# Blockwise-causal attention and routed experts on one core: q and k cast by their loads into a two-head layout, v loaded per head, first expert computed block by block

## The chip, the cores and the metric

The kernel runs on 1 core of one Trainium2 chip. The metric is device time in microseconds (us), as the median of several runs: 352.87 us over 3 runs (350.46 to 354.48) before the change. A core has these engines: TensorE (PE; its weight loads are listed as PEld), VectorE (DVE), ScalarE (ACT), GpSimd (POOL) and SyncE (SP). Transfers between memory (DRAM) and the on-chip SBUF are issued by SP, ACT or POOL and run on 16 DMA engines. A load that also changes the data type is issued by POOL here. TensorE writes to PSUM, from where DVE or ACT take results.

## The reference, cut to what matters

```python
# q, k, v: (8, 8, 576, 64) float32;  batch, heads, positions, head size
scores = matmul(q, k.transpose(0, 1, 3, 2)) / sqrt(64)
mask = (pos[:, None] // 64) >= (pos[None, :] // 64)        # causal by blocks of 64
attn = softmax(where(mask, scores, -1e9))
x = matmul(attn, v)                                        # rows: (batch, position); 8 heads x 64 = 512 columns
# 4608 rows x, domain_id: one of 8 experts per row
for e in range(8):
    rows = domain_id == e
    out[rows] = relu(x[rows] @ w1[e]) @ w2[e]              # w1: 512 x 1024, w2: 1024 x 512, float32
```

All inputs are float32; the kernel computes in float16 with float32 accumulation.

## The kernel before, in words

The program has two stages, each written out in the order in which its instructions are issued (manual schedule; every engine runs its own instructions in that order and waits only for the data and buffers that an instruction needs).

**Attention** (L457 to L546) walks over 32 head pairs, `p` = 0 to 31, four pairs to a batch. `emit_T(p)` (L323) transposes q and k of a pair: 16 PE transposes into one PSUM tile PT, then two DVE copies into the SBUF tile QK (L334 for q, L337 for k). It is called two pairs ahead. `emit_G` (L368) computes transposed scores in three groups, each followed by exponentials on ACT (L366): group 0 is `mm_qk` for the first 128 keys, group 1 the second and fourth, group 2 the third plus twelve small 64x64 matmuls (L388) for the diagonal blocks. `emit_P` and `emit_Q` (L424, L429) multiply with v for the pair before, at L414 and L419; DVE divides by the row sums (L435, L436) and writes the rows x. The sums come from columns of ones in the v tiles `vS` and `VE` (`emit_VE`, L442). After the fourth pair of a batch `store_x` (L449) writes 576 rows to the DRAM tensor `x_rows` over SP.

A partition holds four consecutive positions of a head (1 KB of float32), 128 partitions hold 512 positions. The other 64 positions of q (the first) and of k (the last) are "tails", loaded separately into `ts` and transposed once per batch (`emit_tail`, L343). With four positions per partition, the order of positions inside QK is permuted, and `inverse` (L189) computes permuted row numbers for the gather (the tile `rw`).

Loads arrive as float32 in `qs`, `ks`, `ts` and `vst`, and are then cast to float16 tiles `qh`, `kh`, `th`, `vS`. For batch 0 DVE and ACT cast q, k and tails, and DVE casts v. For all others POOL does (`cast_qk` L111, `cast_t` L118, `cast_v` L132; the casts have the lines L116, L120 and L134). `loads(p)` (L470) places these casts and the next loads on POOL, for two batches at a time, after pair p; the staging tiles have room for two batches, so a load of two batches waits until those before are cast. POOL also issues weights: expert 0 (w1 and w2) after pair 3, w1 of expert 1 after pair 19. A generator `routing()` (L273) interleaves, in chunks after the pairs, the DVE and PE work that finds the rows of each expert (L212 and L220 among it).

**Experts** (L549 to L645): for each of 8 experts, 5 blocks of 128 rows are gathered from `x_rows` by POOL (L556), transposed by PE (L568), multiplied with w1 (`mm1`, L582: 64 matmuls of 320 columns; ReLU on ACT, L588), then with w2 (`mm2`, L597), copied by DVE (L601) and scattered to the output by POOL (L602). Gathers run two experts ahead. Weights are cast by their loads (L139, L142). The gather of the first block waits for the last `x_rows` store. A loop for overflowing experts follows; it isn't entered with these inputs.

## Time and profile before

| what | value |
|---|---|
| median of 3 runs | 352.87 us (350.46 to 354.48) |
| the profiled execution | 349.14 us |
| its span (first to last instruction of the trace) | 347.1 us, 2.04 us less |
| mean granted TensorE clock | 0.888 |
| busy: PE, PEld | 277.5 us (80%), 177.8 us (51%) |
| busy: POOL | 213.5 us (62%) |
| busy: DVE, ACT | 165.8 us (48%), 141.4 us (41%) |
| moved by DMA | 65.03 MB, 187 GB/s over the span |
| read from memory | 67.15 MB |

The profile shows one execution. Busy time is a share of the whole span, over two stages with different limits, so a stage is read by itself: the page cuts the span into 40 slices of 8.7 us with one digit each (tenths of busy time; the clock in tenths; the DMA engines' mean share), and the trace can be asked for any stretch. Bytes moved are counted as written, so a load that casts float32 to float16 counts half of what it reads. A group row gives line, engine, operation, output and input tiles, shapes and count, then busy us and mean ns, then the idle time of the engine just before it. A row in order of time begins with the start and the duration in us; durations of matmuls overlap, and the distance from start to start is what one costs. In a row of waits stand the total, the number of times and the longest.

### The profile page before, as it was taken

How to read it: one execution, taken by the hardware profiler on the slowest of the kernel's cores; microseconds unless marked ns; L12 is line 12 of the kernel's file. 1: busy time of each engine (PE TensorE's matmuls, PEld its weight loads, DVE VectorE, ACT ScalarE, POOL GpSimd, SP SyncE). 2: the span in 40 equal slices, each digit the busy share in tenths (PEclk: the TensorE clock that was granted, in tenths of full speed). 3: DMA queues.
4: the chain of work that ended last, by engine and by line, in shares of the span. 5: the costliest groups of instructions: out<-in, count | busy, mean ns of one | idle time of the engine just before them, and what ended most of it. 6: DMA issues, size and time to landing. Idle time of an engine off the chain costs nothing. (4 is left out here: it accounts for less than half of the span.)

```text
span 347.1 us, 7286 instructions
## 1 busy us (share of the span) xinstructions
PE 277.5 (80%) x3014; PEld 177.8 (51%) x3014; DVE 165.8 (48%) x315; ACT 141.4 (41%) x196; POOL 213.5 (62%) x252
## 2 busy tenths in 40 slices
PE   1567661797977986998329999999999999999990
PEld 1345441565655654765215556474656556564740
DVE  6874991759777783876210332404041322313030
ACT  2544551347474983999203314060513224050500
POOL 9858992975668575100068578887878687703141
PEclk9996885559788996999857999999999999999996
DMA  7999999999938999122225999899998989601121
GB/s 217 250 283 266 313 188 247 190 328 272 266 93 284 274 263 235 27 73 70 68 75 113 195 246 212 241 191 240 180 259 181 255 168 226 213 14 69 66 92 50
DMA packets 29539, 65.03 MB, mean 187 GB/s; under 512 B 4734, under 2 KB 11390, under 8 KB 29504
## 3 DMA queue, kind: packets, MB, share of 16 engines
q0 software_dynamic: 21328, 57.42, 67.7%
q1 hardware_dynamic: 7376, 6.72, 7.0%
q8 instruction: 25, 0.41, 0.5%
q10 hardware_dynamic: 800, 0.39, 0.4%
q14 instruction: 10, 0.08, 0.1%
HBM read 67.15 MB, written 15.20 MB: 237 GB/s over the span
## 5 line engine op out<-in xcount | busy, mean ns | idle before, releaser
L366 ACT ACTIVATE A<-ps 128x1024 f16<-128x1024 f32 (+1 forms) x96 | 82.6, 885 | 67.4 <-PE ps L361 40.8
L588 ACT ACTIVATE hT<-ph 128x640 f16<-128x640 f32 x64 | 45.1, 704 | 118.2 <-PE ph L582 118.2
L582 PE MATMUL ph<-xT,w1h 128*128 128x320 f16 x512 | 72.7, 303 | 0.2 <-DVE xT L571 0.2
L597 PE MATMUL po<-w2h,hT 128*128 128x512 f16 x320 | 70.4, 379 | 0.0
L556 POOL DMA_INDIRECT xg<-x_rows,tok x40 | 40.5, 1012 | 47.4 <-DMA x_rows<-x 34.5
L602 POOL DMA_INDIRECT out_dram<-osb,tok x40 | 40.8, 1020 | 39.7 <-DVE osb L601 26.1
L582 PEld LDWEIGHTS <-w1h 128*128 128x128 f16 x512 | 50.7, 99 | 22.0 <-issue 0.6
L601 DVE COPY osb<-po 128x512 f32<-128x512 f32 x40 | 27.7, 691 | 50.4 <-PE po L597 49.3
L571 DVE COPY xT<-pt 128x512 f16<-128x512 f16 x40 | 15.7, 421 | 73.6 <-PE pt L568 71.4
L597 PEld LDWEIGHTS <-hT 128*128 128x128 f16 x320 | 30.9, 98 | 36.0
L414 PE MATMUL po<-VE,ATE 128*128 128x130 f16 x160 | 34.6, 241 | 18.0 <-DVE x L436 15.2
L419 PEld LDWEIGHTS <-A 128*128 128x128 f16 x640 | 34.3, 107 | 16.9 <-issue 15.9
L361 PE MATMUL ps<-QK 64*128 64x512 f16 (+3 forms) x256 | 39.3, 346 | 1.2 <-ACT ATE L366 0.7
L419 PE MATMUL po<-vS,A 128*128 128x65 f16 x640 | 39.2, 208 | 0.0
L436 DVE TENSOR_TENSOR x<-po,rc 128x768 f16<-128x768 f32 x32 | 30.6, 957 | 3.3 <-DMA x_rows<-x 2.2
L126 POOL DMA_DIRECT2D vst<-in_v_dram x25 | 25.1, 1014 | 10.5 <-DMA qs<-in_q_dram 9.1
L568 PE MATMUL pt<-identh,xg 128*128 128x128 f16 x160 | 15.0, 229 | 14.9 <-issue 9.3
L330 PE MATMUL PT<-identh,qh 128*64 128x128 f16 x256 | 16.1, 261 | 10.7 <-DVE qh L116 8.6
L134 POOL CAST vS<-vst 128x1024 f16<-128x1024 f32 (+1 forms) x21 | 18.2, 897 | 10.0 <-DMA vst<-in_v_dram 7.0
L142 POOL DMA_DIRECT2D w2h<-in_moe_w_dram x32 | 17.4, 562 | 9.2 <-DMA vst<-in_v_dram 6.2
L337 DVE COPY QK<-PT 128x512 f16<-128x512 f16 x32 | 21.8, 680 | 0.0
L414 PEld LDWEIGHTS <-ATE 128*128 128x128 f16 x160 | 16.5, 103 | 10.1 <-issue 7.8
(103 smaller groups left out, 288.7 us busy)
## 6 DMA issues: line engine op xcount, KB each, us to landing
w1h<-in_moe_w_dram POOLq DMA_DIRECT2D x32, 256.0 KB, 6.7
w2h<-in_moe_w_dram POOLq DMA_DIRECT2D x32, 256.0 KB, 7.7
qs<-in_q_dram POOLq DMA_DIRECT2D x3, 2048.0 KB, 11.7
ks<-in_k_dram POOLq DMA_DIRECT2D x3, 2048.0 KB, 18.0
vst<-in_v_dram POOLq DMA_DIRECT2D x12, 512.0 KB, 21.7
x_rows<-x SPq DMA_DIRECT2D x8, 512.0 KB, 8.4
vst<-in_v_dram POOLq DMA_DIRECT2D x11, 256.0 KB, 13.1
qs<-in_q_dram POOLq DMA_DIRECT2D x1, 1024.0 KB, 9.8
```

Source lines behind the costliest of these rows:

```text
L126: nc.gpsimd.dma_start(out=vst[0:n, c, o, :], in_=v[b0:b1, :, 128 * c : 128 * c + n, :].rearrange("b h p d -> p (b h) d"))
L361: nc.tensor.matmul(out=o[:, i], lhsT=QK[h, 1, 128 * c : 128 * c + 128], rhs=QK[h, 0, 128 * c : 512], start=True, stop=True)
L366: nc.scalar.activation(out=o, in_=i, func=AF.Exp, scale=0.125)
L414: nc.tensor.matmul(out=o[:, 1:131], lhsT=st["AE"][:, 128 * m : 128 * m + 128], rhs=VE[b % 2][:, m, hp, 1:131], start=True, stop=(m == 0))
L419: nc.tensor.matmul(out=o[:, 1 + 65 * i : 66 + 65 * i], lhsT=at_block(st, i, c, m), rhs=vS[b % 3][:, c, hp, 1 + 65 * i : 66 + 65 * i], star ...
L436: nc.vector.tensor_tensor(out=st["x"][:, :, 128 * hp : 128 * hp + 128].rearrange("p (b w) (i z) -> p b w i z", b=2, i=2), in0=pv[:, :, :, ...
L556: nc.gpsimd.indirect_dma_start(out=g[:, blk, :], out_offset=None, in_=xd, in_offset=bass.IndirectOffsetOnAxis(ap=tok[:, 1, blk : blk + 1], ...
L582: nc.tensor.matmul(out=ph[:, i, 0:hw], lhsT=w1h[:, dc].rearrange("p (c n r) -> p c r n", n=128, r=2)[:, fc // 2, fc % 2], rhs=xT[:, dc, hw ...
L588: nc.scalar.activation(out=hT[:, fc].rearrange("p (i n) -> p i n", i=2), in_=ph[:, :, 0:hw], func=AF.Relu)
L597: nc.tensor.matmul(out=po[:], lhsT=hT[:, fc, 128 * blk : 128 * blk + 128], rhs=w2h[:, fc, :], start=(fc == 0), stop=(fc == 7))
L601: nc.vector.tensor_copy(out=osb[:], in_=po[:])
L602: nc.gpsimd.indirect_dma_start(out=dst[blk], out_offset=bass.IndirectOffsetOnAxis(ap=tok[:, 0, blk : blk + 1], axis=0), in_=osb[:], in_off ...
```

## The change

1. **q and k are cast by their loads** and lie otherwise. `qs`, `ks`, `ts`, their casts, the tails and `emit_tail` are gone. One head of a pair lies in partitions 0 to 63, the other in 64 to 127; a partition holds nine consecutive positions (2304 bytes of float32, 1152 of float16), so 64 partitions hold all 576. Four POOL loads per batch (q and k, two halves of the partitions). Batch 0 comes in two pieces, its first pair ahead of everything.
2. **`emit_T`** transposes 64x64 pieces: 36 per pair instead of 16, in two PSUM tiles (q, then k), each with one DVE copy of 576 columns that puts positions in natural order. The tail operands of `emit_G` go away, `mm_qk` reads q from column 64 on, and the permuted row numbers in `inverse` go.
3. **v** has three staging tiles of one batch. A batch is loaded head by head, eight loads of 512 positions and one of the last 64 positions of all heads; v of batch 0 is loaded by SP. Casts stay on POOL.
4. **`loads(p)`** goes batch by batch: q and k, four heads of v, the cast of the v before, four more heads. The weights of experts 0 and 1, w2 of expert 1 included, follow the last batch.
5. **The last `x_rows` store** is split: 384 columns after pair 30, 128 after pair 31, the larger part of the latter on ACT's queue.
6. **Expert 0** is computed per block of 128 rows: `transpose_mm1` transposes block n+1, then does 32 matmuls of 128 columns on block n, with one ReLU of 1024 columns; 160 weight loads and matmuls in place of 64.

The order on POOL, before, from the load of batches 2 and 3 on (names: `qs`, `ks`, `ts`, `vst` are staging tiles, `qh_..`, `kh_..`, `th_..`, `vS_..` the float16 tiles):

```order
L126 DMA vst<-in_v_dram 128x16x64 x4
L126 DMA vst<-in_v_dram 64x16x64
L116 CAST qh_75<-qs 128x1024 x2
L116 CAST qh_76<-qs 128x1024 x2
L116 CAST kh_79<-ks 128x1024 x2
L116 CAST kh_80<-ks 128x1024 x2
L139 DMA w1h<-in_moe_w_dram 128x1024 x4
L142 DMA w2h<-in_moe_w_dram 128x1024 x4
L120 CAST th_83<-ts 128x512
L134 CAST vS_87<-vst 128x8x128 x2
L134 CAST vS_87<-vst 64x4x128
```

And with the change, from the load of batch 3 on (`qh_72`, `kh_76` are now written by the load itself):

```order
L69 DMA qh_72<-in_q_dram 64x4x576 x2
L69 DMA kh_76<-in_k_dram 64x4x576 x2
L102 DMA vst_77<-in_v_dram 128x4x64 x4
L112 CAST vS_82<-vst_79 128x8x128 x2
L112 CAST vS_82<-vst_79 64x4x128
L102 DMA vst_77<-in_v_dram 128x4x64 x4
L106 DMA vst_77<-in_v_dram 64x8x64
L69 DMA qh_69<-in_q_dram 64x4x576 x2
```

The casts of q, k and tails no longer stand between two loads, and the weights no longer stand ahead of the later batches.

The order on DVE around pairs 1 and 2, before (QK and QT are the transposed operands, `rc` the reciprocals, the rows from L256 on a routing chunk):

```order
L337 COPY QK<-PT 128x512
L435 RECIPROCAL rc<-po 128x12
L436 TENSOR_TENSOR x<-po,rc 128x6x128
L350 COPY QT<-PT 128x4x64
L353 COPY QT<-PT 128x4x64
L256 CAST rit<-rank 128x36
L258 TENSOR_SCALAR hit<-rit 128x36
```

And with the change:

```order
L294 COPY QK<-PT 128x576 x2
L374 RECIPROCAL rc<-po 128x12
L375 TENSOR_TENSOR x<-po,rc 128x6x128
L215 CAST rit<-rank 128x36
L217 TENSOR_SCALAR hit<-rit 128x36
```

Both copies of a pair are of one strided form now, and the two tail copies per batch are gone; the routing chunks stand where they stood.

The diff, cut to its core:

```diff
-    qs = asb.tile([128, 16, 256], F32, name="qs")
-    ks = asb.tile([128, 16, 256], F32, name="ks")
-    ts = asb.tile([128, 16, D], F32, name="ts")
-    vst = asb.tile([128, 5, 16, D], F32, name="vst")
-    qh = [asb.tile([128, H, 256], F16, name=f"qh{i}") for i in range(4)]
-    kh = [asb.tile([128, H, 256], F16, name=f"kh{i}") for i in range(4)]
-    th = [asb.tile([128, H, D], F16, name=f"th{i}") for i in range(4)]
+    qh = [asb.tile([128, HP, S], F16, name=f"qh{i}") for i in range(4)]
+    kh = [asb.tile([128, HP, S], F16, name=f"kh{i}") for i in range(4)]
+    vst = [asb.tile([128, 5, H, D], F32, name=f"vst{i}") for i in range(3)]
...
+    def load_qk(b, g0=0, g1=HP):
+        for src, dst in ((q, qh), (k, kh)):
+            for i in range(2):
+                nc.gpsimd.dma_start(
+                    out=dst[b % 4][64 * i : 64 * i + 64, g0:g1, :],
+                    in_=src[b].rearrange("(g i) (p j) d -> i p g (j d)", i=2, j=9)[
+                        i, :, g0:g1, :])
+    load_qk(0, 0, 1)
...
+    for c in range(5):
+        n = min(128, S - 128 * c)
+        nc.sync.dma_start(
+            out=vst[0][0:n, c], in_=v[0, :, 128 * c : 128 * c + n, :].rearrange(
+                "h p d -> p h d"))
     identh = const.tile([128, 128], F16, name="identh")
     make_identity(nc, identh[:])
+    load_qk(0, 1, HP)
+    load_qk(1)
...
+    def load_v(b, h0, h1):
+        for h in range(h0, h1):
             nc.gpsimd.dma_start(
+                out=vst[b % 3][:, 0:4, h, :],
+                in_=v[b, h, 0:512, :].rearrange("(c p) d -> p c d", p=128))
+        if h1 == H:
+            nc.gpsimd.dma_start(
+                out=vst[b % 3][0:64, 4],
+                in_=v[b, :, 512:S, :].rearrange("h p d -> p h d"))
...
     def emit_T(p):
         b, hp = divmod(p, HP)
-        PT = aps.tile([128, 2, 4, 128], F16, name="PT", tag="PT", bufs=2)
-        QK = asb.tile([128, 2, 512], F16, name="QK", tag="QK", bufs=3)
+        QK = asb.tile([128, 2, S], F16, name="QK", tag="QK", bufs=3)
         for s, src in enumerate((qh[b % 4], kh[b % 4])):
-            for j in range(4):
+            PT = aps.tile([128, 9, 64], F16, name="PT", tag="PT", bufs=2)
+            for j in range(9):
                 for i in range(2):
+                    h = slice(64 * i, 64 * i + 64)
                     nc.tensor.transpose(
-                        out=PT[64 * i : 64 * i + 64, s, j, :],
-                        in_=src[:, 2 * hp + i, 64 * j : 64 * j + 64],
-                        identity=identh[:])
+                        out=PT[h, j],
+                        in_=src[h, hp, 64 * j : 64 * j + 64],
+                        identity=identh[h, h])
+            nc.vector.tensor_copy(
+                out=QK[:, s].rearrange("p (n j) -> p n j", j=9),
+                in_=PT[:].rearrange("p j n -> p n j"))
...
+        for b in range(2, B):
+            if p == max(0, 4 * b - 10):
+                load_qk(b)
+                load_v(b, 0, 4)
+                cast_v(fn, b - 1)
+                load_v(b, 4, H)
+        if p == 4 * B - 12:
+            w1s[0], t1 = load_w1(wsb, 2, moe_w1[0])
+            w2s[0], t2 = load_w2(wsb, 2, moe_w2[0])
+            for f in t1:
                 f()
+            cast_v(fn, B - 1)
+            for f in t2:
+                f()
+        if p == 4 * B - 10:
+            w1s[1], t1 = load_w1(wsb, 2, moe_w1[1])
+            w2s[1], t2 = load_w2(wsb, 2, moe_w2[1])
+            for f in t1 + t2:
                 f()
...
+            if prev["p"] == npair - 2:
+                store_x(prev, 0, DM - 128, nc.sync)
+            elif prev["p"] == npair - 1:
+                store_x(prev, DM - 128, DM, nc.scalar)
+            elif prev["p"] % HP == HP - 1:
+                store_x(prev, 0, DM, nc.sync)
...
+    def transpose_mm1(g, w1h):
+        xT = msb.tile([128, 4, CAP], F16, name="xT", tag="xT", bufs=2)
+        hT = msb.tile([128, 8, CAP], F16, name="hT", tag="hT", bufs=2)
+        transpose_block(g, xT, 0)
+        for blk in range(NB):
+            if blk + 1 < NB:
+                transpose_block(g, xT, blk + 1)
+            n = slice(128 * blk, 128 * blk + 128)
+            ph = mps.tile([128, 2, 512], F32, name="ph", tag="ph", bufs=2)
+            pv = ph[:].rearrange("p a (f n) -> p (a f) n", n=128)
+            for fc in range(8):
+                for dc in range(4):
+                    nc.tensor.matmul(
+                        out=pv[:, fc], lhsT=w1_cols(w1h, dc, fc), rhs=xT[:, dc, n],
+                        start=(dc == 0), stop=(dc == 3))
+            nc.scalar.activation(out=hT[:, :, n], in_=pv, func=AF.Relu)
+        return hT
```

177 lines of the change are left out of this document (29 added, 148 removed).

## The prediction

> **What bounds the kernel now.** I read the 40 slices first, then the table by stretches, then the waits, then the order in time of single pairs and loads.
>
> ```profile
> span 347.1 us, 7286 instructions
> PE   1567661797977986998329999999999999999990
> PEclk9996885559788996999857999999999999999996
> DMA  7999999999938999122225999899998989601121
> ```
>
> From slice 22 on (190 us) PE is at 9 in every slice: that is the expert stage, eight experts, and it is bound by TensorE. Before slice 20 PE swings between 5 and 9, its clock drops to half, and DMA stands at 9 until slice 16. The table by stretches (time, busy us of PE, PEld, DVE, ACT, POOL, clock, DMA share, GB/s) separates the two conditions of the attention stage:
>
> ```profile
> 50.00:60.00 10.00, 2.55 (x39) 1.95 (x38) 3.42 (x6) 0.98 (x2) 3.88 (x8) 0.55 1.06 242
> 150.00:160.00 10.00, 9.73 (x206) 7.11 (x207) 8.65 (x18) 9.49 (x14) 0.00 (x0) 1.00 0.02 6
> ```
>
> At 50 to 60 us every compute engine is idle most of the time while the DMA engines are full: attention starves for input. At 150 to 160 us all input is in and ACT (9.49 of 10) and PE set the pace. The waits agree: of ACT's idle time the most, 40.8 us in 24 waits, is for the scores of PE, up to 9.6 at once.
>
> ```profile
> ACT A L366 <- PE ps L361: 40.8, 24, 9.6
> ```
>
> Each head pair ends with the DVE multiply L436, so its rows give the pace (start, duration):
>
> ```profile
> 22.99 0.96 DVE L436 TENSOR_TENSOR x<-po,rc 128x768 f16<-128x768 f32 x1
> ...
> 151.99 0.96 DVE L436 TENSOR_TENSOR x<-po,rc 128x768 f16<-128x768 f32 x1
> ...
> 155.05 0.96 DVE L436 TENSOR_TENSOR x<-po,rc 128x768 f16<-128x768 f32 x1
> ...
> 169.46 0.96 DVE L436 TENSOR_TENSOR x<-po,rc 128x768 f16<-128x768 f32 x1
> ```
>
> Pair 0 is done at 23.95, pair 31 at 170.42: 146.5 us for 31 pairs, 4.7 each, where an unstarved pair takes 3.06. So some 51 us of the stage are starvation, and what the change does to the loads decides the result.
>
> **The loads.** One-microsecond stretches in which one kind of transfer ran nearly alone:
>
> ```profile
> 64.00:65.00 1.00, 1.00 (x13) 0.59 (x12) 1.00 (x1) 0.49 (x2) 1.00 (x3) 0.50 1.10 205
> 113.00:114.00 1.00, 0.90 (x21) 0.76 (x17) 0.99 (x3) 1.00 (x2) 0.00 (x0) 1.00 1.01 344
> 120.00:121.00 1.00, 1.00 (x28) 0.84 (x26) 0.16 (x2) 0.81 (x2) 0.29 (x1) 1.00 1.02 148
> 125.00:126.00 1.00, 1.00 (x22) 0.62 (x21) 0.96 (x2) 1.00 (x3) 1.00 (x2) 1.00 1.07 280
> ```
>
> They are weights that the load casts (205 GB/s counted in the f16 that is written, so 410 in the f32 that is read), plain q/k in runs of 1 KB (344), the tails ts, 256-byte runs into 64 partitions (148), and v, 256-byte runs into 128 partitions (280). Now per batch q and k are 2.36 MB of f32 and land as 1.18 MB of f16, in four loads into 64 partitions each. No row shows a cast load into 64 partitions. Ends: at best the weights' rate, 1.18/0.205 = 5.8 us; at worst it is f32 at the tails' rate, 2.36/0.148 = 15.9. The halves cost what bytes written cost: ts against v is 0.53 with equal runs. Half of the 1-KB row gives 172 GB/s written (2.3 KB runs read, 1.15 written, nearest to it): 6.9 us. v: 1.18/0.28 = 4.2 us a batch; the x store, 0.59 MB, taken at v's rate, 2.1. Sum 13.2 us a batch; the tails and the weights of expert 0, which stood ahead of batches 4 and 5, are gone from the middle.
>
> POOL issues all of it and casts v (start, us, work):
>
> ```profile
> 6.43 4.53 POOL L126 DMA_DIRECT2D vst<-in_v_dram  x5
> ...
> 20.95 0.69 POOL L126 DMA_DIRECT2D vst<-in_v_dram  x1 [1.85 <-DMA qs<-in_q_dram]
> ...
> 60.72 0.53 POOL L142 DMA_DIRECT2D w2h<-in_moe_w_dram  x1 [0.44 <-DMA vst<-in_v_dram]
> ...
> 61.80 2.57 POOL L134 CAST vS<-vst 128x1024 f16<-128x1024 f32 x3
> ```
>
> A load of 512 runs costs 0.69 us (the one at 20.95), of 128 runs 0.53. Nine v loads of 512 runs are 6.2, four q/k loads of 256 runs about 0.6 each 2.4, the v cast 2.6: 11.2 us a batch. It stays under the DMA's 13.2, and the casts of q, k and th leave POOL and the path. So loading runs at 13.2 us a batch: 2 us start, 11 for batch 0, 7 x 13.2, last batch in at about 105.
>
> **PE and ACT per pair.** The steady pair, PE alone:
>
> ```profile
> 153.05 0.23 PE L414 MATMUL po<-VE,ATE 128*128 128x130 f16 x1
> ...
> 153.69 0.28 PE L361 MATMUL ps<-QK 64*128 64x256 f16 x2
> 153.91 0.22 PE L388 MATMUL ps<-QT,QK 64*64 64x64 f16 x2
> ...
> 154.21 0.23 PE L414 MATMUL po<-VE,ATE 128*128 128x130 f16 x1
> ...
> 154.68 0.39 PE L361 MATMUL ps<-QK 64*128 64x512 f16 x2
> 155.00 0.41 PE L330 MATMUL PT<-identh,qh 128*64 128x128 f16 x8
> ...
> 155.57 0.39 PE L361 MATMUL ps<-QK 64*128 64x384 f16 x4
> ```
>
> From start to start: scores 0.32, transposes 0.57, the next scores as much as the first, 0.32, P 0.64, G2 0.52, Q 0.47: 2.84 us under ACT's 3.03 to 3.06. The 16 transposes go; 36 of 64x64 come. The nearest row is L388: twelve 64x64 matmuls, alternating between the same two quarters of the array, from 153.91 to 154.21, 25 ns each. 36 x 25 = 0.90, and 0.09 for the change of shape as now (16 x 30 ns of 0.57): 0.99. PE: 2.84 - 0.57 + 0.99 = 3.26 us a pair, so PE instead of ACT sets the unstarved pace. Ends: two at a time would be 0.45 + 0.09, PE 2.8 and ACT's 3.03 stays; at two and a half times the row, 62 ns, PE would need 4.6, today's starved pace.
>
> [...]
>
> **DVE, and the routing.** Groups of DVE in the attention stage (busy us, mean ns):
>
> ```profile
> L436 DVE TENSOR_TENSOR x<-po,rc 128x768 f16<-128x768 f32 x32 | 30.6, 957 | 3.3 <-DMA x_rows<-x 2.2
> L337 DVE COPY QK<-PT 128x512 f16<-128x512 f16 x32 | 21.8, 680 | 0.0
> L334 DVE COPY QK<-PT 128x512 f16<-128x512 f16 x32 | 13.4, 418 | 7.4 <-PE PT L330 7.3
> L445 DVE COPY VE<-vS 64x1280 f16<-64x1280 f16 x16 | 12.1, 754 | 0.1
> L212 DVE TENSOR_TENSOR L<-iota_x,lo_h 128x1152 f16<-128x1152 f16 x4 | 9.9, 2486 | 0.0
> L435 DVE RECIPROCAL rc<-po 128x12 f32<-128x12 f32 x32 | 7.3, 229 | 25.8 <-PE po L414 25.8
> L350 DVE COPY QT<-PT 128x256 f16<-128x256 f16 x8 | 3.3, 415 | 8.1 <-PE PT L346 8.1
> ```
>
> and, on PE, one of the two halves of the routing's gather product:
>
> ```profile
> 88.70 4.11 PE L220 MATMUL PT<-Hh,L 128*128 128x120 f16 x18
> ```
>
> L350 and L337 are one kind of strided copy: 265 ns more for 256 more elements. The two copies of a pair become two of that kind with 576, so 0.75 us each (680 and 64 more at 1.04 ns). DVE per pair: 1.50 + 0.23 + 0.96 + 0.38 for VE (two of 0.754 per four pairs) = 3.07, under PE's 3.26. But the routing's chunks, after pairs 1 to 12, come on top. On DVE I take 11 us for them, an estimate: L212's 9.9 are the largest part and should shrink, since its four are of one size and a mean of 2.5 us must come from waiting beside POOL's casts, of which fewer stay. On PE they are twice the 4.11 us of L220. DVE 3.07 + 0.92 = 3.99, PE 3.26 + 8.2/12 = 3.94: I take 4.0 for pairs 1 to 12 and 3.26 for 13 to 31. Beside each other they hide; one behind the other it would be 4.7, 8 us more, which the range holds. The clock should stay up, as no idle stretch of several us remains.
>
> **The sum of the stage.** Pair 0: DVE loses three casts and two tail copies and gains 0.4 in each of four copy pairs, and v is asked for some 4 us earlier, by SP: I take 22 for 23.95. Then 12 x 4.0 = 48 and 19 x 3.26 = 62: last pair at 132 instead of 170.42, -38.4. Loads, at 105 plus four pairs and the tail, would allow 121; they hide. The weights of experts 0 and 1 (4.2 MB written, 20 us at 205 GB/s) are issued behind batch 7, from 105 to some 125, before they are needed; if loading were late, they would run into the stores and gathers.
>
> **Between the stages.** The last store must land before the first gather:
>
> ```profile
> 174.72 1.10 POOL L556 DMA_INDIRECT xg<-x_rows,tok  x1 [34.53 <-DMA x_rows<-x]
> 176.12 1.02 POOL L556 DMA_INDIRECT xg<-x_rows,tok  x1 [0.30 <-issue]
> ...
> 178.38 0.35 PEld L568 LDWEIGHTS <-xg 128*128 128x128 f16 x4 [9.38 <-issue]
> ...
> 196.37 8.80 PE L597 MATMUL po<-w2h,hT 128*128 128x512 f16 x40
> 205.00 8.86 PE L582 MATMUL ph<-xT,w1h 128*128 128x320 f16 x64
> 213.69 0.61 PE L568 MATMUL pt<-identh,xg 128*128 128x128 f16 x8
> ```
>
> 170.42 to 174.72 is issue and landing; three quarters of that store now leave a pair earlier, on two queues: -1. Expert 0's first product then waits for two gathered blocks instead of five, three gathers of 1.3 us, so about 3 us less; but it costs 160 weight loads and matmuls of 128 columns for 64 of 320. At 60 to 76 ns (eight in 0.61, the latency of one counted whole) that is 9.6 to 12.2 us against 8.86: -2 to 0. If each cost what one of the 64 costs now, 138 ns, 22: +10. The transposes are the nearer row, by width: I take -2, since blocks still wait for their gathers part of the time. From expert 0's second product (196.37) to the end, 150.7 us, nothing changes: expert 1's w2 arrives earlier, but PE did not wait for it.
>
> Span: 132 + 23 + 150.7 = 305.7; the profiled execution took 349.14 on a span of 347.1, so 307.7 on that footing, -41.4. The median of the three runs, 352.87, is 1.1% above that execution: 311.
>
> **Rivals.** *Second, ACT keeps the pace* (0.17): transposes of the two halves run together and the routing hides. 22 + 31 x 3.03 + 4 = 120, total 299. For it: the two quarters are independent; against: L388 shows 25 ns with the same alternation. *Third, the loads still bind* (0.14): writing 64 partitions halves the cast rate itself, 103 GB/s, 11.5 us, 17.8 a batch: last batch in at 143, pair 31 at 159, total 338. For it the ts row, against it that a cast writes half the bytes per byte read. *Fourth, slower than before* (0.04): the f32 bytes count, 148 GB/s, 15.9 us for q and k, 22.2 a batch: last batch at 177, pair 31 at 193, total 373. It decides from 19.7 us a batch, 13.4 of it for q and k, under 176 GB/s of f32. *Fifth, no change* (0.03): the transposes cost as much as was won. With 4.6 us a pair, that is 62 ns for each of the 36, pair 31 is near 172 and the total 351. For it: 1152 instead of 512 of them, each with its own weight load; against: the 25 ns of L388. [...]
>
> **How the numbers follow.** The forecast has 0.62, with its own range 300 to 322. The range 290 to 338 takes in the second and third. A measurement can tell about 1% from no change: faster by more than that 0.93 (first three cases), same 0.03, slower 0.04.
>
> **What would show it.** Right: L436 rows 3.2 to 3.3 us apart in the last 19 pairs, with PE and not ACT full; no stretch of the stage with PE under 5; the clock at 1.00; 64 QK copies of 0.75 us; last pair near 132; q/k loads near 170 GB/s; 160 matmuls of expert 0 at about 60 ns. Wrong: PE idle for q/k or v with the DMA share at 1 after batch 1 (third or fourth case), transposes over 40 ns, or POOL never waiting and always late with v.

## The result and the profile after

The change made the kernel faster, by much less than forecast: 340.32 us (median of four runs, 337.4 to 344.02) against 352.72 us for the kernel before beside it, a ratio of 0.9624 with a 95% interval of 0.9514 to 0.9734. The forecast was 311.0 us with a range of 290 to 338. The profiled execution took 338.54 us on a span of 336.8.

The changed kernel was run twice more in the experiments: 347.89 us (ratio 0.9879, 0.9715 to 1.0043) and 328.01 us (0.9407, 0.9365 to 0.9448). These are three sets of runs, each with the kernel before beside it on one chip (352.72, 353.77 and 349.14 us). Ratios and intervals leave out executions more than 1.5% above the fastest of their kernel, so they differ a little from quotients of the medians. What differs between the sets lies behind the attention stage and is told below. To separate it from the change I show the first profile and, beside it, the one of the third set (same_third, span 323.8).

| stretch, us | before | forecast | after | same_third |
|---|---|---|---|---|
| end of pair 0 (x written) | 23.95 | 22 | 28.55 | 28.05 |
| pairs 1 to 12 | 81.90 | 48 | 57.17 | 58.28 |
| pairs 13 to 31 | 64.57 | 62 | 61.05 | 61.32 |
| last x to expert 0's second product | 25.95 | 23 | 28.42 | 20.56 |
| from there to the issue of the last scatter | 143.22 | 143.2 | 149.22 | 143.23 |
| from there to the end | 7.51 | 7.5 | 12.39 | 12.36 |
| span | 347.1 | 305.7 | 336.8 | 323.8 |

The page of the changed kernel: the 40 slices that were shown of before.

```profile
span 336.8 us, 8696 instructions
PE   1278699999999989817659979999898999999940
PEclk9999978987999979985978999999999999999985
DMA  8999999979997994223694968969699794102030
```

From slice 5 to slice 16 PE is now nearly always at 8 or 9, where it swung between 1 and 9 before (the prediction's "between 5 and 9" overlooked the 1 at 50 to 60 us, and its "DMA stands at 9 until slice 16" the 3 and 8 of slices 11 and 12). Stretches of the attention stage (time; busy us of PE, PEld, DVE, ACT, POOL; clock; DMA share; GB/s):

```profile
50.00:60.00 10.00, 9.92 (x150) 6.85 (x142) 6.79 (x11) 4.74 (x6) 10.00 (x14) 0.83 1.11 219
100.00:110.00 10.00, 9.66 (x254) 7.04 (x252) 8.67 (x15) 9.09 (x14) 5.59 (x10) 1.00 0.83 159
```

At 50 to 60 us PE was busy for 2.55 of 10 us before; the wait for input is gone. POOL has no free time there now. The pairs, by the multiply that ends each (L375, was L436):

```profile
27.59 0.96 DVE L375 TENSOR_TENSOR x<-po,rc 128x768 f16<-128x768 f32 x1
...
103.53 0.96 DVE L375 TENSOR_TENSOR x<-po,rc 128x768 f16<-128x768 f32 x1
107.01 0.96 DVE L375 TENSOR_TENSOR x<-po,rc 128x768 f16<-128x768 f32 x1
...
145.81 0.96 DVE L375 TENSOR_TENSOR x<-po,rc 128x768 f16<-128x768 f32 x1
```

The first stands 4.6 us later than before and the last 23.7 us earlier. Behind the attention, expert 0's first product, block by block (L515), is meant to run through:

```profile
158.57 1.99 PE L515 MATMUL ph<-xT,w1h 128*128 128x128 f16 x29
...
161.30 0.33 PE L515 MATMUL ph<-xT,w1h 128*128 128x128 f16 x3 [0.74 <-issue]
161.34 0.42 DVE L489 COPY xT<-pt 128x512 f16<-128x512 f16 x1 [5.94 <-remote]
...
164.15 1.89 PE L515 MATMUL ph<-xT,w1h 128*128 128x128 f16 x31 [1.03 <-issue]
164.39 1.02 ACT L518 ACTIVATE hT<-ph 128x1024 f16<-128x1024 f32 x1 [3.33 <-PE pt L486]
...
172.47 1.02 ACT L518 ACTIVATE hT<-ph 128x1024 f16<-128x1024 f32 x1 [3.36 <-remote]
173.20 0.42 DVE L489 COPY xT<-pt 128x512 f16<-128x512 f16 x1 [6.47 <-remote]
```

There are two holes, 160.6 to 164.2 and 170.3 to 173.7 us. By the profile, which models the ends of matmuls, PE was done with what ACT and DVE wait for 2 to 3 us before these start. The semaphore records of the trace, which no view lists, say where that time lies: the signal on which DVE starts at 161.34 us came from PE at 161.32, and the one for ACT at 172.47 came at 172.45. So PE's signal is late, and ACT and DVE follow it at once. The same code in same_third:

```profile
158.60 1.95 PE L515 MATMUL ph<-xT,w1h 128*128 128x128 f16 x32
...
160.61 1.95 PE L515 MATMUL ph<-xT,w1h 128*128 128x128 f16 x32
...
162.62 3.74 PE L515 MATMUL ph<-xT,w1h 128*128 128x128 f16 x64
...
168.21 2.97 PE L542 MATMUL po<-w2h,hT 128*128 128x512 f16 x13
```

No hole: from block 1 on 128 matmuls at 58 to 61 ns each, and the second product 20.6 us after the last x. POOL's gathers lie at the same place there (150.9 to 162.8 us; 150.1 to 161.9 in the first profile), so that they lie beside the blocks doesn't make the holes by itself.

### The profile page after: what moved, and what is told of

Its sections match the earlier page's. It is cut to its first block, busy times and chain, and to the rows that moved or that the text cites. A ratio compares the mean times of both kernels' runs of the same rounds, so it can differ in the third digit from the quotient of the medians.

```text
span 336.8 us, 8696 instructions
## 1 busy us (share of the span) xinstructions
PE 276.2 (82%) x3718; PEld 182.5 (54%) x3718; DVE 161.4 (48%) x290; ACT 138.4 (41%) x190; POOL 210.3 (62%) x275
## 5 line engine op out<-in xcount | busy, mean ns | idle before, releaser
L533 ACT ACTIVATE hT<-ph 128x640 f16<-128x640 f32 x56 | 39.4, 704 | 102.6 <-PE ph L528 97.7
L542 PE MATMUL po<-w2h,hT 128*128 128x512 f16 x320 | 73.1, 387 | 1.5 <-DVE osb L546 1.3
L528 PE MATMUL ph<-xT,w1h 128*128 128x320 f16 x448 | 62.0, 299 | 0.0
L528 PEld LDWEIGHTS <-w1h 128*128 128x128 f16 x448 | 43.8, 98 | 18.1
L546 DVE COPY osb<-po 128x512 f32<-128x512 f32 x40 | 27.6, 691 | 47.0 <-PE po L542 45.9
L294 DVE COPY QK<-PT 128x576 f16<-128x576 f16 x64 | 46.5, 791 | 4.2 <-PE PT L290 3.9
L102 POOL DMA_DIRECT2D vst<-in_v_dram x56 | 42.6, 773 | 3.2 <-DMA vst<-in_v_dram 1.6
L358 PE MATMUL po<-vS,A 128*128 128x65 f16 x640 | 36.5, 201 | 0.0
L375 DVE TENSOR_TENSOR x<-po,rc 128x768 f16<-128x768 f32 x32 | 30.6, 958 | 1.2
L290 PE MATMUL PT<-identh,qh 64*64 64x64 f16 x576 | 16.8, 204 | 12.5 <-DMA qh<-in_q_dram 6.1
L290 PEld LDWEIGHTS <-qh 64*64 64x64 f16 x576 | 13.8, 117 | 20.3 <-issue 13.4
L486 PEld LDWEIGHTS <-xg 128*128 128x128 f16 x160 | 11.3, 103 | 20.6 <-issue 19.4
```

The lines of the kernel that those rows point to most:

```text
L102: nc.gpsimd.dma_start(out=vst[b % 3][:, 0:4, h, :], in_=v[b, h, 0:512, :].rearrange("(c p) d -> p c d", p=128))
L290: nc.tensor.transpose(out=PT[h, j], in_=src[h, hp, 64 * j : 64 * j + 64], identity=identh[h, h])
L294: nc.vector.tensor_copy(out=QK[:, s].rearrange("p (n j) -> p n j", j=9), in_=PT[:].rearrange("p j n -> p n j"))
L358: nc.tensor.matmul(out=o[:, 1 + 65 * i : 66 + 65 * i], lhsT=at_block(st, i, c, m), rhs=vS[b % 3][:, c, hp, 1 + 65 * i : 66 + 65 * i], star ...
L528: nc.tensor.matmul(out=ph[:, i, 0:hw], lhsT=w1_cols(w1h, dc, fc), rhs=xT[:, dc, hw * i : hw * i + hw], start=(dc == 0), stop=(dc == 3))
L533: nc.scalar.activation(out=hT[:, fc].rearrange("p (i n) -> p i n", i=2), in_=ph[:, :, 0:hw], func=AF.Relu)
```

## The experiments

The runs were made in five sets. In two of them (the kernel before 349.66 and 349.14 us) every kernel of the changed family took 143.2 us from expert 0's second product to the last scatter; I call these sets even. In the other three (350.74, 352.51, 353.77) and in the first result they took 147 to 154 us. Kernels are compared within a set, by their profiles' stretches where the times scatter too much.

**First set: four single edits.**

*whole_expert0*, expert 0 as the kernel before does it:

```
+    xT = transpose_x(xgs[0])
     for e in range(E):
-        hT = mm1(xT, w1s[e]) if e else transpose_mm1(xgs[0], w1s[0])
+        hT = mm1(xT, w1s[e])
```

> The changed kernel with expert 0 as before: its five transposes of the gathered blocks first, then its first product over 640 columns at once. Theory (the block-by-block form of expert 0 loses): from the last x row to expert 0's second product 25 us instead of 28.4, no holes of 3 us on PE between, and a span 3 us shorter than the changed kernel's 336.8, about 334, the rest of the trace unchanged. Rival (the holes at 160 and 170 us come from what POOL and the DMA engines do in that time, gathers and weights, whatever PE's order): holes of the same size in the first product of expert 0, the stretch stays at 28 us or grows by the 2 us that the overlap of transposes and products was to save, total 340 to 343.

335.85 us (0.9691, 0.9563 to 0.9819), span 334.2; 25.43 us to the second product. The theory's numbers came: the other three of this set, with the block form, took 27.9 to 28.6 us to the second product, so the form cost 3 us here. That it always does was wrong (see together and iota_by_act).

*constants_first*, `load_qk(0, 1, HP)` and `load_qk(1)` moved behind the four constants of POOL:

> The changed kernel with POOL's constants (triangle, three iotas) issued ahead of the twelve load issues that stand before them. Theory (pair 0 waits for the constants): the routing's first product starts at about 10 us instead of 15, x of pair 0 starts at 22 to 23 instead of 27.6, nothing behind it gets longer, last x row 141 to 142 instead of 145.8, total about 5 us less (335). Rival (the loads come 3 to 4 us later and become the wait): pair 0 gains 4 us but pairs 1 to 4 lose 3 of them to the loads of batches 0 and 1, last x row 145, total 339 to 340.

344.67 us (0.9885, 0.9578 to 1.0193). x of pair 0 at 28.2 us: nothing gained. The routing's first product did come at 10.55 us, but pair 1's k now landed late:

```profile
17.36 0.26 PE L290 MATMUL PT<-identh,kh 64*64 64x64 f16 x1 [2.43 <-DMA kh<-in_k_dram]
18.45 0.68 PE L290 MATMUL PT<-identh,kh 64*64 64x64 f16 x17 [0.83 <-DMA kh<-in_k_dram]
```

The wait had moved whole, from the constants to the loads behind them.

*v_by_chunks*, the inner loop of `load_v`:

```
-        for h in range(h0, h1):
+        for c in range(5 * h0 // H, 5 * h1 // H):
             nc.gpsimd.dma_start(
-                out=vst[b % 3][:, 0:4, h, :], ...
+                out=vst[b % 3][0:n, c], ...
```

> The changed kernel with v of batches 1 to 7 loaded by five loads per batch, one for each 128 positions with all heads, as before, instead of one per head. Theory (loads stop binding after batch 1, so their form does not matter): POOL issues 10 loads less per batch or about 3 us less, the pairs keep their pitch of 3.0 to 3.1 us from pair 13 on, last x row within 1 us of 145.8, total within 1% of 340. Rival (the loads per head are what lets the pairs run at 3 us): batches come 2 us later each, last x row 150 to 155, total 347 to 350.

343.02 us (0.989, 0.9729 to 1.0051). Last x ended at 151.3 us, where the other three of this set stood at 148.0, 151.7 and 150.0; pairs 13 to 31 took 63.0 us, 62.9 with whole_expert0. The edit takes four load issues from a batch, nine to five, and not the ten of the expectation. The rival's price of 2 us per batch did not appear, so the form of v's loads is at most a small part of the gain.

*contiguous_L*, the weights of the routing's matmuls laid out side by side:

```
-            L = sb.tile([128, 128, NH], F16, name="L", tag="L")
+            L = sb.tile([128, NH, 128], F16, name="L", tag="L")
-                nc.tensor.matmul(out=pv, lhsT=L[:, :, j], rhs=Hh[:, :, :, j],
+                nc.tensor.matmul(out=pv, lhsT=L[:, j], rhs=Hh[:, :, :, j],
```

> The changed kernel with the routing's operand L laid out so that each of the 36 routing matmuls loads 128 adjacent columns as weights, instead of every 18th. Theory (the stride of the weights makes a routing matmul cost 228 ns, and TensorE's granted clock falls after it): 18 of them take 2 us or less instead of 4.1, the clock stays above 0.8 behind them, the two long pairs of 8.1 and 8.7 us shrink to 5 or 6, total 5 us less. Rival (the moving operand with its stride of 18 sets the 228 ns): 18 matmuls still take 4.1 us, the long pairs stay, total within 1% of 340.

343.49 us (0.9791, 0.9415 to 1.0167). Eighteen routing matmuls still took 4.05 us, the long pairs 8.4 and 8.4 us: the rival. DVE paid for it, 1.77 us per L operation for 1.00.

**Second set: the next four.**

*w2_late*: whole_expert0, and `load_w2(..., moe_w2[1])` moved behind the attention as before.

> The changed kernel with the whole second stage of before: expert 0 not block by block, and w2 of expert 1 loaded after the attention into the pool of four buffers. In the changed kernel expert 0's second product to the last scatter's issue takes 149.2 us (before: 143.2), with DVE's copies starting 1 us late and PE waiting beside POOL's gathers. Theory (the place of the gathers on POOL against PE's transposes sets that: four loads of w2 less ahead of them put each gather beside the next expert's transposes): this stretch goes back to 143 or 144 us, and the program's total falls to about 330. Rival (it comes from where PE's stream of instructions has grown or shrunk, which the weights do not change): the stretch stays at 148 us as with expert 0 undone alone, total 335. Neither says what sets the 12.4 us from the last scatter to the end (7.5 before); if that is tied to the same place it falls too.

336.12 us (0.9552, 0.9494 to 0.961). From expert 0's second product to expert 5's it took 97.7 us; before 96.7, the changed kernel 102.5, whole_expert0 101.6. Every second product took 8.80 us and every group of transposes 2.18, as before, and none of POOL's gathers lay beside the transposes of experts 1 to 7. That fits the theory for this part. The whole stretch to the last scatter, however, took 150.2 us and not its 143 to 144: one first product, expert 6's, took 6 us more, with PE idle and then at half clock. The profiled execution took 340.08 us, 4 more than the median; the median itself is nearer to the rival's 335 than to the theory's 330. The tail stayed at 12.5 us, so it is another matter.

*small_constants_first*: triangle and small iotas ahead of the loads, the 4.29-us iota behind them.

> The changed kernel with the triangle and the two small iotas (0.9 us on POOL) ahead of the loads of batch 0's other pairs and of batch 1, and the 4.29-us iota behind these. With all constants first the wait went to the loads of pair 1 (k at 17.4 and 18.5 us), so theory now: both waits were the one iota of 4.29 us, and here neither the routing's operand nor pair 1's k waits for it; first product of the routing at 10 us, x of pair 0 at 22 to 23.5 us instead of 27.6, last x row 4 us earlier in a run whose other pairs take the same. Rival (DVE, busy for 16.4 of 17 us in pairs 1 to 4, is the bound there and only changes its order): pair 0 gains 4 us, pairs 1 to 4 lose 3 of them.

341.81 us (0.9693, 0.9632 to 0.9753), x of pair 0 still at 27.6: the iota began at 10.05 us, 0.1 us after DVE's cast, which took 4.53 us. The wait is not the place in POOL's order but the overlap with DVE, as in the changed kernel:

```profile
10.11 4.29 POOL L97 IOTA iota_x<- 128x2304 f16 x1
...
10.09 4.39 DVE L233 CAST iota_h<-iota_i 128x128 f16<-128x128 int32 x1 [0.23 <-POOL iota_i L91]
10.23 4.25 DVE L234 CAST p_f<-p_i 128x1 f32<-128x1 int32 x1
```

*contiguous_H*, the moving operand side by side instead (with the broadcasts that write it turned round):

```
-            Hh = sb.tile([128, 3, ncols, NH], F16, name="Hh", tag="Hh")
+            Hh = sb.tile([128, NH, 3, ncols], F16, name="Hh", tag="Hh")
-                nc.tensor.matmul(out=pv, lhsT=L[:, :, j], rhs=Hh[:, :, :, j],
+                nc.tensor.matmul(out=pv, lhsT=L[:, :, j], rhs=Hh[:, j],
```

> The changed kernel with the routing's moving operand laid out with its 120 columns adjacent instead of 18 elements apart. Adjacent weights left 18 routing matmuls at 4.05 us (228 ns each). Theory (the stride of the moving columns sets it): 18 take 1.0 to 2.0 us, and if the fall of TensorE's clock to 0.50 behind them comes from their slowness, it stays above 0.8 and the two long pairs of 8 us shrink to about 5, 5 us in all. Rival (each such matmul waits for something else than its operands' layout, as the clock's fall already begins inside them): they stay at 4.1 us and the pairs at 8 us.

339.79 us (0.9622, 0.9553 to 0.969). The theory on the stride held; rows of the changed kernel and of this one:

```profile
52.19 4.12 PE L194 MATMUL PT<-Hh,L 128*128 128x120 f16 x18
```

```profile
53.71 1.28 PE L194 MATMUL PT<-Hh,L 128*128 128x120 f16 x18
```

228 ns became 71. But the long pairs only went to 6.6 and 5.2 us. DVE paid here too, 0.90 us per operation on H for 0.52. Pairs 1 to 12 took 56.4 us; w2_late and small_constants_first, of this set, 58.2 and 58.4. The same edit in together and act_iota_and_H left the first long pair at 9.2 and 8.2 us, with a copy of VE on DVE of 3.0 and 2.1 us in it (0.95 here), and brought the second to 4.9 and 5.2. So the first pair's length is not PE's lump alone.

*v_cast_by_load*: `load_v` writes `vS` (four tiles) in fp16, the casts of v on POOL go.

> The changed kernel with v of batches 1 to 7 cast by its loads, straight into the tile that the products read (four of it), so that POOL casts nothing. Theory (POOL's casts stretch DVE's instructions, 0.94 us per copy of QK in pairs 1 to 6 against 0.75 later): copies of QK go back to 0.71 to 0.76 in all of the attention, pairs 1 to 12 take 3 to 5 us less, last x row about 141 to 143. Rival (written in rows of 128 bytes, v's loads take twice as long and become the wait): batches come every 15 us or more, pairs beyond 13 show waits for vS on PE, last x row 150 or later.

336.39 us (0.9567, 0.9512 to 0.9621). Groups of DVE between 28 and 86 us (busy us, mean ns), first same_third, then this kernel:

```profile
L294 DVE COPY QK<-PT 128x576 f16<-128x576 f16 x24 | 18.0, 859 | 1.0 <-PE PT L290 0.9
...
L384 DVE COPY VE<-vS 64x1280 f16<-64x1280 f16 x6 | 5.5, 925 | 0.0
...
L166 DVE TENSOR_SCALAR ub<-u_f,base_f 128x36 f16<-128x36 f32 x1 | 3.1, 3097 | 0.0
...
L263 DVE TENSOR_SCALAR cnt<-inc 128x8 f32<-128x8 f32 x1 | 2.6, 2582 | 0.0
```

```profile
L295 DVE COPY QK<-PT 128x576 f16<-128x576 f16 x28 | 19.8, 749 | 1.7 <-PE PT L291 1.7
...
L385 DVE COPY VE<-vS 64x1280 f16<-64x1280 f16 x6 | 3.1, 524 | 0.1
```

Beside POOL's casts an operation on 8 columns took 2.6 us in same_third; the same one took 0.23 in this kernel. Without POOL's casts pairs 1 to 12 took 52.0 us, 4 to 6 less than in the other three of this set. Then the rival's time came: pairs 13 to 31 took 68.0 us (63.1 to 64.3), with the DMA share at 1.20 between 90 and 120 us, 0.98 in same_third. But not the way it was argued: nowhere in these pairs does PE wait for v. PE stands for 7.7 us in seven stops without a wait, of the kind shown in the last section; the other three of the set have 2.4 to 3.8 us of them, same_third 3.0. Last x ended at 148.5, so most was given back.

**Third set, an even one.**

*iota_by_act*: the small constants first, and

```
-    nc.gpsimd.iota(out=iota_x[:], ...)
+    nc.scalar.copy(out=iota_x[:],
+                   in_=iota_h[:].unsqueeze(2).to_broadcast([128, 128, NH]))
```

> The changed kernel with the small constants ahead of the loads and the 4.29-us iota gone from POOL: ACT, idle until the first scores, builds the same table by a broadcast copy. In the run with the small constants first the iota began at 10.05 us, just as DVE's three casts at 9.95 did, and these again took 4.2 to 4.5 us. Theory (the iota on POOL stretches DVE's casts from 0.2 to 4.4 us, and the first scores wait for them): casts at 10 us take 0.1 to 0.3 us, first scores at 11 to 12 us instead of 15.7, x of pair 0 at 22.5 to 24 us instead of 27.6, and the following pairs as before, so 4 us less up to the last x row of runs that are otherwise alike (143 to 146). Rival (pair 0 then waits for v or for pair 1's loads): x of pair 0 no earlier than 26.

328.2 us (0.9414, 0.9381 to 0.9448). DVE's casts:

```profile
10.29 0.22 DVE L231 CAST iota_h<-iota_i 128x128 f16<-128x128 int32 x1
10.42 0.15 DVE L233 CAST p_f<-p_i 128x1 f32<-128x1 int32 x1
```

The cause of the late start is shown: 4.39 us became 0.22 and x of pair 0 came at 25.2, a little late of the theory. It took 20.77 us to the second product without any edit there, which opened the question of the sets.

*together*: whole_expert0, w2_late, contiguous_H and iota_by_act in one.

> The changed kernel with expert 0 whole, w2 of expert 1 loaded late as before, the routing's moving operand contiguous, and the table built by ACT. Theory (the four costs add): last x row ends at 140 to 144, expert 0's second product 25.4 us after that, 143 to 144 us from there to the last scatter, 12.4 us to the end: span 321 to 326, time 323 to 329, ratio to before 0.92 to 0.935. Rival (attention is bound by something that fills each gap again, as pair 1's loads did): last x row still at 147 to 150, time 331 to 334.

331.86 us (0.9496, 0.9455 to 0.9537): the rival, and slower than iota_by_act alone, by 3.7 us. Last x ended at 146.9 as there (146.4), and expert 0 as a whole took 24.75 us for 20.77. Where no holes are, block by block is worth 4 us.

*no_loop*: the loop `For_i(0, n_it, 1)` taken out.

> The changed kernel without the loop at its end, which runs no round on this input (left out: the rounds for experts with more rows than five blocks, so the kernel is right for this input alone). From the last scatter's issue to the end the changed kernel takes 12.4 us, the kernel before 7.5. Theory (the end is spent around the loop: reading the count, the branch over its body, and fetching the code behind it): 3 to 5 us are left. Rival (it is the last scatter's landing and the program's end): 10 us or more stay.

322.42 us (0.9237, 0.919 to 0.9284). Issue of the last scatter, in the changed kernel and here:

```profile
324.41 0.98 POOL L547 DMA_INDIRECT out_dram<-osb,tok  x1 [0.74 <-DVEq L592]
```

```profile
311.73 0.98 POOL L547 DMA_INDIRECT out_dram<-osb,tok  x1 [0.75 <-DVE osb L546]
```

With spans of 336.8 and 319.4 that leaves 12.4 and 7.7 us: the loop, which runs no round, costs 4.7. More than the theory's 3 to 5 us stay. What stays can be seen in the records of POOL's sequencer, which the views leave out: its last DRAIN instruction takes 5.54 us in the changed kernel (6.76 here) and 1.46 before, and the instruction INC_SWDGE_SEM ahead of it 1.53 for 0.53. Together that is 5.1 us more, the whole of the longer tail. The drain changes only where POOL's loads are changed: 6.44 us in v_by_chunks, 5.29 in v_cast_by_load, 9.13 in qk_plain, 5.54 in every other run that keeps the loop. What it waits for is not shown.

*qk_plain*: q and k of batches 2 to 7 staged in fp32 through SP's queue and cast by POOL, in the new layout.

> The changed kernel with q and k of batches 2 to 7 loaded in fp32 by SP's queue into a staging tile, in the same layout, and cast by POOL as before, v staged in two tiles instead of three. Theory (the cast by the load is what freed the pairs: POOL gets 4.5 us of casts more per batch and loses 2.5 us of issues, DVE is stretched beside them, and the loads move no less from DRAM): pairs 5 to 31 take 3.5 to 4 us instead of 3.0 to 3.2, last x row 155 to 165, total 350. Rival (the layout alone, one head per 64 partitions and no tails, was enough, since POOL has 2 us per batch left and the loads are hidden): last x row 145 to 150, total within 1% of 340.

367.37 us (1.0549, 1.0503 to 1.0596): slower than the kernel before, and beyond the theory. Last x ended at 184.2. POOL's groups between 45 and 150 us:

```profile
L127 POOL CAST vS<-vst 128x1024 f16<-128x1024 f32 (+1 forms) x16 | 14.7, 948 | 0.0
L87 POOL CAST qh<-qst 128x1152 f16<-128x1152 f32 x12 | 13.4, 1152 | 14.7 <-DMA qst<-in_q_dram 14.7
L87 POOL CAST kh<-kst 128x1152 f16<-128x1152 f32 x12 | 13.4, 1144 | 2.9 <-DMA kst<-in_k_dram 2.9
```

26.8 us of casts came back, and POOL, in order, stood 14.7 us for one load of q. The loads also stand behind the x stores on SP's queue here and v has a tile less, so the 37 us are not the cast's alone. PE also stands for 8.1 us without a wait between pairs 13 and 31. So the run points to the cast in the load as what carries the gain, but several things changed at once.

**Fourth set: is it the kernel or the set?**

*same_again*: the changed kernel.

> The changed kernel itself, unchanged, beside the next three on one chip. Theory (the holes belong to the kernel as it is built: where its instructions lie, or POOL's order): 28 us from the last x row to expert 0's second product, 148 to 149 us from there to the last scatter, 12.4 us to the end, 337 to 344 in all. Rival (they belong to the chip or the set of runs): 21 us and 143 us as in the two kernels without holes, about 328 in all.

347.89 us; 28.83 and 150.5 us, 12.4 at the end. The holes came again, in the changed kernel, beside kernels that show them too.

*act_iota_and_H*:

> The iota built by ACT together with the contiguous moving operand of the routing, the rest as in the changed kernel. Theory (the gains of pair 0 and of the routing's matmuls add): last x row 2 to 4 us before the 145.4 of the run with ACT's iota alone, total 324 to 327. Rival (what PE gives back DVE takes, 0.38 us more for each of four operations, in pairs where DVE is full): last x row 145 to 146, total 328 again.

341.37 us (0.9742, 0.9572 to 0.9912). Last x ended at 147.06 us, in same_again at 150.14: 3 us, of the size of the theory, but in one profile each. The total says nothing of it, as 25.7 and 154.3 us follow.

*w2_late_alone*:

> The changed kernel with only w2 of expert 1 loaded after the attention as before; expert 0 stays block by block. Theory (POOL's order against PE's transposes makes the holes and the late copies): 21 to 23 us to expert 0's second product, 143 to 144 us from there to the last scatter. Rival (where the instructions lie makes them, and POOL's order does not): 28 and 148 us. If the changed kernel beside it shows no holes either, this run can tell nothing of them.

339.63 us (0.97, 0.9576 to 0.9825); 26.85 and 149.65 us: neither. Expert 0's second product was back at 8.79 us, the next five took 9.7 to 10.2. So neither w2 late alone (here) nor expert 0 whole alone (the first set: 25.43 and 148.4 us) brought both stretches back in an uneven set.

*before_no_loop*:

> The kernel before without the loop at its end (left out: the rounds for experts with more rows than five blocks, none on this input). Its end takes 7.5 us from the last scatter's issue; the changed kernel's took 12.4, and 7.7 without the loop. Theory (the loop's branch and count cost 4 to 5 us in the changed kernel only, since in the one before the code behind it is at hand): 7 us stay here, total within 1% of before. Rival (the loop costs both the same): 3 us are left, total 4 us less.

350.41 us (0.9968, 0.9891 to 1.0045), 4.1 us at the end for 7.5: the rival, the loop costs 3.4 us here. That is by the profiles; the total doesn't resolve it. So 1.3 of the changed kernel's 4.9 us of longer tail go with the loop and 3.6 are there without it (POOL's last DRAIN: 6.76 us in no_loop, 3.58 here). In its profile, too, signals of PE are late against the modelled end of the work, the latest by 3.75 us, and ACT, the row of 307.17, follows that one at once:

```profile
307.17 1.30 ACT L588 ACTIVATE hT<-ph 128x640 f16<-128x640 f32 x2 [15.92 <-remote]
307.93 4.42 PE L582 MATMUL ph<-xT,w1h 128*128 128x320 f16 x16 [4.58 <-ACT hT L588]
```

**Fifth set, an even one.** *same_third* is the changed kernel, *iota_by_act_again* the edit beside it.

> The changed kernel itself once more, beside the iota built by ACT. If the long stretches hang on the set of runs, both kernels of this set show them or neither does: 28 and 149 us, total 338 to 348, or 21 and 143 us, total about 330. If they belong to the kernel as it is built, this one shows them whatever the other does.

> The iota built by ACT once more. Theory (the gain of this edit by itself is what pair 0 gains, 2.4 us in the profiles, and the rest of the 0.941 came with the set of runs): 2 to 3 us, 0.7%, less than the changed kernel beside it. Rival (the edit also mends the long stretches): 10 us or more less than the changed kernel, with 21 and 143 us where that has 28 and 149.

328.01 us (0.9407, 0.9365 to 0.9448) and 328.2 us (0.9402, 0.9367 to 0.9436): the same. Both show 143.2 us, and 20.6 and 22.2 us ahead of it. So the holes hang on the set, and iota_by_act's fine result in the third set was that of its set. x of pair 0 came at 24.9 instead of 27.1 us; at pair 12 the two stood at 85.6 and 85.4.

No version is shown to beat the changed kernel in both kinds of sets. In the uneven ones w2_late has the best ratio, 0.955, but v_cast_by_load of the same set stands at 0.957, which is not apart from it, and the changed kernel was not run in that set; in the even ones nothing that keeps the loop does better than the change itself.

## Why the prediction was wrong, point by point

The direction and the mechanism were right: the loads stopped starving the pairs. The size was wrong. The step that failed most is "Beside each other they hide" (point 3, 9 to 10 us); beside it the iota's new place was missing (point 2, 6 us), and "nothing changes" behind the second product did not hold (point 7, 5 to 11 us). Against the forecast span of 305.7 us the profile is 31.1 us longer, same_third 18.1. By the table's stretches:

1. **Loads: right.** q and k were to be written at 172 GB/s (6.9 us a batch). Without the first and last tenth of its packets, a batch was written at 186 to 200 GB/s in the changed kernel and at 160 to 195 in same_third; as a whole it took 7.3 to 10.3 us, since other loads ran beside it. The last batch was to be in at 105 us: its last v was issued at 99.6 and landed at 102.8. So the third rival's 338 us, near the measured median, was not what happened: no stretch after batch 1 shows PE idle for q or k. qk_plain points to the cast in the load as what carries this.

2. **Pair 0: +6.1 to +6.6 us, a step that was missing.** I counted DVE's work and v's load, not that the 4.29-us iota moves from 2.2 to 10.1 us, beside the casts that DVE makes for the routing. iota_by_act shows it. But mended, it brought nothing by pair 12; the work behind took it back.

3. **Pairs 1 to 12: +9.2 to +10.3 us, the step "Beside each other they hide".** 4.0 us a pair took the routing as spread evenly and DVE's 11 us for it as free of POOL. DVE was in fact full in pairs 1 to 4, here in same_third:

```profile
28.00:45.00 17.00, 12.37 (x293) 9.12 (x288) 16.44 (x31) 10.34 (x14) 17.00 (x23) 0.90 1.01 199
```

16.44 us of 17, and POOL all of it. Without POOL's casts of v pairs 1 to 12 take 4 to 6 us less (v_cast_by_load). I had taken fewer casts on POOL for little stretching. For the operation L that was right, 1.00 us for 2.49; but the casts of v still lie beside the routing and stretch its other operations. The other part is the two lumps of 18 matmuls, in each of which ACT gets no scores: 4.1 us each, and 8 us or more for their pairs. contiguous_H took 5.7 us of PE's work away and gained 2. How the 9 to 10 us divide between the two is not shown beyond these two edits, which were not run together.

4. **The clock "should stay up": wrong.** It falls just behind the first lump and inside the second, in stretches in which PE is busy throughout: the lumps ran from 52.2 to 56.3 and from 71.4 to 75.5 us, and the clock was at half from 56.6 to 60.0 and from 73.7 to 80.5. After the first:

```profile
57.50:60.00 2.50, 2.50 (x42) 1.71 (x37) 1.20 (x2) 1.27 (x2) 2.50 (x5) 0.50 0.94 207
```

The trace of before has half clock behind such a lump too, at 92 to 99 us behind the one of 88.70; I had put all of it down to starving. In contiguous_H, with lumps of 1.28 us, half clock comes at 57.8 to 61.2 us, behind about 1.4 us in which PE had no work, and not behind the second lump.

5. **Pairs 13 to 31: 61.1 to 61.3 us for 62, by luck.** The step "PE instead of ACT sets the unstarved pace" failed. A steady pair of the changed kernel:

```profile
109.63 0.39 PE L302 MATMUL ps<-QK 64*128 64x512 f16 x2
109.95 0.47 PE L290 MATMUL PT<-identh,qh 64*64 64x64 f16 x18
110.26 0.45 PE L290 MATMUL PT<-identh,kh 64*64 64x64 f16 x18
110.64 0.39 PE L302 MATMUL ps<-QK 64*128 64x384 f16 x4
```

From 109.95 to 110.64 the 36 transposes cost 0.69 us, for a forecast of 0.99. They start in twos, 3 ns apart, a two every 32 ns. So do the rows of L388 that I took as the nearest: my 25 ns there counted the change of shape, which the sum then added once more. With 0.69, PE has 2.84 - 0.57 + 0.69 = 2.96 us a pair, and the pace stays with ACT: the steady pairs are 3.00 us apart, as in the second rival. Pairs 29 and 30, with no transposes beside them, are 3.00 apart too, though PE is busy for only 2.1 to 2.4 us of each. That the stage took as long as forecast comes from longer pairs between them, each fourth one of 3.5 us and single ones of up to 5.1 (that one holds the stop of PE of the last section). The copies of QK took 0.75 us, as said.

6. **Between the stages: 28.4 or 20.6 us for 23.** In the even sets the -2 us of the block form was too careful: whole against block by block is 24.75 against 20.77 us. In the uneven ones the holes take it and 3 us more.

7. **"From expert 0's second product to the end, nothing changes": wrong by the tail, 4.9 us in every set,** and by 6 us behind late signals in the first profile (4 to 11 in the uneven sets). 1.3 us of the tail go with the loop. The tail's length lies in POOL's last DRAIN and the instruction ahead of it (5.1 us more than before), and it changes with POOL's loads; what is drained is not shown.

What the uneven sets differ in stays open. Their profiles of the changed family have 4 to 16 signals of PE that come 0.5 to 4.1 us after the modelled end of the work; those of the even sets have none. ACT and DVE start 0.02 us behind the signal in most cases, and never more than 0.42 us behind a late one. Transfers don't take longer: packets of 2048 bytes took 189 to 197 ns on average in the uneven sets and 188 to 191 in the even ones. The second set, uneven, and the third, even, ran on a chip of the same number, so the chip alone doesn't decide. Two rivals were not tried. The uneven profiles also lack 11 to 21 of PE's signals, where the even ones lack none, so the recording itself may take part in what they show. And the place of PE's instructions in memory was not varied by itself. The times of all executions differ, not those of the profiled ones alone: the kernel before differs by about 1% between the sets (349.1 to 353.8 us) and the changed one by 4 to 6%. That POOL's place against PE makes a kernel vulnerable was the theory of w2_late; its profile fits it for five experts, its total does not show it.

## What to carry to other kernels

Move an instruction on POOL only with a look at what DVE does at the new place: the price of the iota and of v's casts was paid on DVE, in operations of 8 to 128 columns that took 2.6 to 4.5 us. Work that came in lumps on the engine between two others cost its lump here (4.1 us of PE, in pairs of 8.1 and 8.7 us), not its mean over the pairs. A cost per instruction is to be read from start to start inside a group of equal ones, since the change of shape at its edge is another cost (18 twos of transposes took 0.69 us, 0.11 more than 18 x 32 ns). And before a stretch of one profile is explained by the kernel, run the same kernel again beside it: 12 us of 340 here came and went with the set of runs.

## What the runs showed of the hardware

**A strided moving operand was slow here, a strided weight operand was not.** 120 moving columns at a stride of 36 bytes took 228 ns, side by side 71; the weights at the same stride cost nothing that shows (4.05 us for 18 without it, 4.12 with it, and the 71 ns are with strided weights).

**DVE's small casts stood still beside POOL's iota.** Three small casts took 4.1 to 4.4 us beside the 4.29-us iota and 0.12 to 0.22 without it. In the changed kernel the three begin at 10.09 to 10.44 us, and all end 0.08 to 0.11 us behind the iota.

**Stops of PE without a wait, and an echo.** In the midst of 18 equal transposes:

```profile
119.68 0.38 PE L290 MATMUL PT<-identh,kh 64*64 64x64 f16 x13
121.17 0.25 PE L290 MATMUL PT<-identh,kh 64*64 64x64 f16 x5 [1.11 <-issue]
```

```profile
122.00:123.00 1.00, 1.00 (x17) 0.91 (x15) 0.22 (x1) 1.00 (x1) 0.00 (x0) 0.50 1.12 209
```

No semaphore, no data: 1.1 us without work, and then 3.4 us at half clock (121.5 to 124.9 us), 2 us lost in a pair that takes 5.1 instead of 3.0. same_third has such a stop of 1.17 us at the same transpose, at 122.4, and its clock stays up, so the half clock doesn't always follow. Numbered in order of start among PE's 7469 recorded instructions (matmuls, weight loads and 33 others), the transpose behind the stop is 4289, which leaves 193 when divided by 256. The 20 kept profiles have 55 stops of over 0.6 us without a wait between 30 and 146 us, the longest of 4.0, and all 55 end at an instruction that leaves 193. The page of the profile shows, under the name of instruction, these transfers:

```profile
q8 instruction: 30, 0.49, 0.6%
```

That is 30 of 16 KB. Each of the 55 stops ends 1.25 to 1.61 us after the end of such a transfer, here of the one from 118.8 to 119.7. These two regularities tie the stops to the transfers; what PE waits for there is not shown. At 17 of the 18 instructions of the changed kernel that leave 193 and lie between 30 and 146 us, PE doesn't stop for over 0.6 us; what makes it stop at the one is not shown either.
